# Attention and a routed expert layer on one core: the beginning of attention is ordered anew (constant rows, sums, zeros on TensorE, DMA semaphores in the plan), and x is turned later

## The chip, the core and the metric

The kernel runs on one core of a Trainium2 chip. It is one launch, and its metric is the device time of that launch in microseconds. The profile names the engines PE (TensorE, with PEld its weight loads), DVE (VectorE), ACT (ScalarE), POOL (GpSimd) and SP (SyncE, which here only issues DMAs).

## What is computed

```python
# attention: q, k, v (8, 8, 576, 64), s (8, 8, 576)
scores = q @ k.T / sqrt(64)
cum = cumsum(maximum(s, 0))
bias = -(cum[:, None] - cum[None, :])
scores = where(causal, -1e9, scores + minimum(bias, 0))
attn = softmax(scores)
x = attn @ v                      # then as (4608, 512)
# expert layer: w_gate (512, 8), w1 (8, 512, 1024), w2 (8, 1024, 512)
logits = x @ w_gate
# in falling order of logits, a token goes to its expert while it has room (576 tokens each)
out[tokens of e] = maximum(x[tokens of e] @ w1[e], 0) @ w2[e]
```

## The kernel before

The work of attention is cut into 16 groups of four heads, and a group into two pairs of heads, so there are 32 pairs, 0 to 31. For each pair there are four stages. The **maximum pass** (`spass`) multiplies q and k roughly on TensorE, and VectorE takes the maximum of each row (L471). The 20 columns of maxima are subtracted on GpSimd (L522), turned on TensorE (L524), copied by ScalarE (L526) and sent by a DMA (L529 on SP, L530 on ScalarE's queue) into rows 67 and 68 of the tile `QK`. The **score pass** (`sts`) multiplies again with these rows as part of the product (L544, L545, L547), so that the exponential on ScalarE (L555) needs no other shift; GpSimd forms the low part of each exponential (L557). `pv` multiplies with v (L621 to L623), `norm` divides, and **turn** transposes x (L684), copies it (L690) and multiplies with the gate's weights (L695, L696). When attention has ended, the tokens are routed and the eight experts run, each with its own weights.

The numbers are kept as two float16 halves. A group's q and k are loaded into `raw` (L382), scaled and rounded by ScalarE (L409, L419), the rest is formed by VectorE (L411), and DMAs move halves between the partitions of `QK` (L416). Rows 64 to 69 of `QK` hold constants and, for each group, the cumulative sums as three float16 digits, here called pieces (`sums`, L346 to L358; the pieces are put into `QK` at L397). `QK` has four slots; group 0 uses slot 0. The constant rows of slots 0 and 1 are filled by VectorE from a small vector that GpSimd makes (L285), those of slots 2 and 3 are copied by a DMA of GpSimd from slot 1 (L290), and a gap in each slot is cleared (L297 on GpSimd or L298 on VectorE). The constants of the router are made by GpSimd (L822 to L851) and at L858 to L860 by VectorE. Until the first data are there TensorE multiplies zeros (L742, `WARM` of them).

The order of the work comes from a planner (`Plan`). Each task is added with an engine, a duration in us, what it depends on and a priority (a lower number goes first); a task may also name buffers of a ring. The planner then plays the work through: it always starts the task that can start earliest, among equals the one with the lowest priority number, and writes the instructions in that order, so each engine's queue has the planned order. A ring with `ordered` set hands out its buffers in the order in which the program asked for them; the three PSUM buffers `pst` of the score pass are such a ring. A DMA's landing is planned from its size, from a shared bus (`KBUS`) and from the constants `BEGIN`, `LAND` and `LATE`. On the chip each DMA that SP or ScalarE issues uses one of eight semaphores in turn, and the issue waits until the DMA that had the semaphore before has landed.

Priorities in pairs' numbers n: maximum pass n - 3 to n - 2, its maxima n - 2.9, score pass n to n + 0.86, `pv` n + 1 to n + 1.9, `turn` n + 2.6, zeros at the beginning 50, constants of the router 3.

Of the kernel before, what the change touches and what calls it, by code (L numbers as in the profile page):

```python
# [14 lines left out]
OP = mybir.AluOpType  # L15
# [24 lines left out]
WARM = 70  # L40
# [49 lines left out]
class Plan:  # L90
# [9 lines left out]
    def __init__(self, t0=0.0):  # L100
# [5 lines left out]
        self.dma = t0  # L106

    def add(self, e, dur, f, deps=(), prio=1, takes=(), uses=(), lat=None, hold=0.0, kb=0, slack=0.0, lock=False,
            alt=None, bulk=False):
# [72 lines left out]
    def start(self, t, x, e):  # L182
# [17 lines left out]
        if x.kb:  # L200

            self.dma = max(self.dma, t + (1.0 if e == "p" else 0.0 if x.land is None else self.BEGIN)) + x.kb / self.KBUS
            x.lat = self.dma - t + (x.lat if x.land is None else x.land + self.LATE[not x.bulk])
        x.end = t + x.lat
        self.free[e] = t + x.occ
# [11 lines left out]
class Attention:  # L217
    def __init__(self, tc, ctx, qT, kT, vN, sN, wg, xs, nb, L, router=None):
# [7 lines left out]
        self.pl = Plan()  # L226
        self.rings()
# [20 lines left out]
    def consts(self):  # L248
# [5 lines left out]
        def P(name, dur, f, prio, deps=(), alt=None):  # L254
            k[name] = pl.add("p", dur, f, [k[d] for d in deps], prio=prio, alt=alt)
# [23 lines left out]
        for i in range(4):  # L279
            t = self.r["QK"].slots[i][0]  # L280
            p0 = -97 if i == 0 else 2 * i - 5.6
            rows, made = t[64:70, 0], []
            if i < 2:
                for c in (1, 0):
                    made.append(pl.add("v", 0.85, lambda rows=rows, c=c: nc.vector.tensor_scalar(  # L285
                        rows[:, c].rearrange("p r (h c) -> p (r h) c", h=2), zrow, self.vec[64:70, c:c + 1], None,
                        op0=OP.add), [k["vec", 0, 4], k["vec", 1, 1], k["mZ"]], prio=p0 if c or i else -94, lock=True))
            else:

                made.append(pl.add("p", 0.9, lambda rows=rows: nc.gpsimd.dma_start(rows, self.r["QK"].slots[1][0][64:70, 0]),  # L290
                                   self.rows1 + [k["QK", 1]], prio=-20, kb=62))
                self.moved.append(made[0])
            k["row", i] = made
            if i == 1:
                self.rows1, self.moved = made, []
# [38 lines left out]
    def sums(self):  # L334
# [12 lines left out]
                    uses=sb)  # L347
        V = lambda dur, f, deps: pl.add("v", dur, f, deps, prio=-95, lock=True, uses=sb)
# [14 lines left out]
    def load(self, g):  # L363
# [22 lines left out]
        if g == 1:  # L386
            fresh = fresh + self.moved
# [17 lines left out]
        for a, z in parts:  # L405
# [4 lines left out]
                         [ld[r, t] for r in range(a, z)] + fresh[:1], prio=t0 - 5 + off + t / 10, uses=[raw, QK]) for t in range(2)]  # L410
# [4 lines left out]
            def move(to, fr, deps, o):  # L415
                return Sy(0.6, lambda d, a=a, z=z: d(part(*to, a, z), part(*fr, a, z)), deps, off=o + off, uses=[QK], kb=72 * n,  # L416
# [1195 lines left out]
```

## Time and profile before

| | |
|---|---|
| median of 3 runs | 755.11 us (754.41 to 755.82) |
| the profiled execution's own time | 760.82 us |
| its span, first to last instruction | 759.1 us |
| mean granted TensorE clock over the span | 0.973 of 2.4 GHz |
| TensorE busy | 719.3 us, 95% |
| VectorE busy | 591.0 us, 78% |
| ScalarE busy | 389.5 us, 51% |
| GpSimd busy | 339.9 us, 45% |
| attention | from 0 to about 318 us |

A row of a timeline gives the start and the length of an instruction in us, its engine, line and operation, the tile that is written and those that are read, the number of merged instructions, and in square brackets how long the engine stood idle before it and what ended that. SPq, ACTq and POOL with DMA_DIRECT2D are issues of DMAs; their length is that of the issue, not of the transfer. A row of a table by stretches gives, for each engine, the busy time and the number of instructions, and then the granted clock (1.00 is 2.4 GHz, 0.50 is 1.2 GHz) and the DMA engines' share.

### The profile page before, as it was taken

What the parts mean: (1) busy time and instruction counts of PE and PEld (TensorE: products, weight loads), DVE (VectorE), ACT (ScalarE), POOL (GpSimd) and SP (SyncE); (2) the same over time, 40 slices, a digit from 0 to 9 for tenths busy, and PEclk for the clock granted to TensorE, in tenths of its full rate; (3) what the DMA queues carried; (4) which work ended last, traced back from release to release, by engine and by line L of the source; (5) the groups of instructions that cost most, each with busy time, mean ns of one, the idle gap of its engine ahead of it and who ended that gap; (6) DMA issues with size and microseconds to landing.
All of it is one profiled execution on the core that took longest, in us unless ns stands there. A gap on an engine that the chain in (4) does not pass through costs nothing.

```text
span 759.1 us, 22699 instructions
## 1 busy us (share of the span) xinstructions
PE 719.3 (95%) x8799; PEld 458.8 (60%) x8799; DVE 591.0 (78%) x1955; ACT 389.5 (51%) x793; POOL 339.9 (45%) x449
## 2 busy tenths in 40 slices
PE   8799999999999999757999999999999999999997
PEld 3467778788888888647645545445455454454444
DVE  8989999999999997878887968879689796260110
ACT  3658888898888878505334414333234332351111
POOL 7667988878788889403031050320312223201102
PEclk9889999999999999858999999999999999999999
DMA  7897768677767431206177383773837749930001
GB/s 231 223 226 190 230 164 240 188 230 200 216 186 215 108 87 65 66 23 218 48 204 186 112 187 113 212 198 115 220 100 167 201 159 240 267 112 32 32 15 50
DMA packets 90838, 119.00 MB, mean 157 GB/s; under 512 B 40350, under 2 KB 56862, under 8 KB 90718
## 3 DMA queue, kind: packets, MB, share of 16 engines
q1 hardware_dynamic: 84172, 98.08, 47.2%
q0 software_dynamic: 6000, 19.01, 8.8%
q8 instruction: 69, 1.13, 0.6%
q10 hardware_dynamic: 558, 0.47, 0.3%
q14 instruction: 39, 0.32, 0.1%
HBM read 71.68 MB, written 19.10 MB: 120 GB/s over the span
## 4 chain that ended last, share of the span: by engine, by line
PE 57%; issue 19%; DVE 15%; POOL 5%; DMA 2%; ACT 1%; SPq 1%; POOLq 0%; another core or an unknown queue 0%; DVEq 0%; ACTq 0%
PE psm L1407 14%; PE psm L1513 12%; DVE pss L471 5%; PE pst L545 4%; PE pst L544 4%; PE pss L502 3%; PE po L621 3%; PE po L623 3%; PE po L622 3%; POOL out_dram L1466 2%; PE psn L1411 2%; DVE QK L411 2%; PE pss L684 2%; PE psa L1084 2%; PE pst L547 1%
## 5 line engine op out<-in xcount | busy, mean ns | idle before, releaser
L557 POOL TENSOR_TENSOR R<-P 128x512 f16<-128x512 f32 (+1 forms) x220 | 219.7, 1024 | 27.5 <-ACT P L555 25.8
L1407 PE MATMUL psm<-xT,w1p 128*128 128x512 f16 (+1 forms) x876 | 194.9, 355 | 0.7 <-ACT xT L1349 0.7
L1513 PE MATMUL psm<-w2p,hT 128*128 128x512 f16 x744 | 169.1, 379 | 0.0
L555 ACT ACTIVATE P<-pst 128x512 f32<-128x512 f32 (+1 forms) x224 | 119.9, 554 | 25.5 <-PE pst L547 10.5
L1411 PE MATMUL psn<-xT,w1p 128*128 128x64 f16 x768 | 129.7, 193 | 0.0
L1466 POOL DMA_INDIRECT out_dram<-y,ids x39 | 39.2, 1004 | 200.7 <-ACT y L1524 175.7
L1407 PEld LDWEIGHTS <-w1p 128*128 128x128 f16 x876 | 80.1, 99 | 78.3 <-issue 0.8
L471 DVE CUSTOM_DVE_ANT_0 pss<-pss,mS 128x512 f32<-128x512 f32 (+3 forms) x256 | 122.8, 507 | 5.7 <-PE pss L502 3.3
L1513 PEld LDWEIGHTS <-hT 128*128 128x128 f16 x744 | 66.8, 98 | 77.4 <-issue 4.3
L621 PE MATMUL po<-V,P 128*128 128x65 f16 x945 | 111.8, 196 | 1.1 <-DVE xp L652 0.9
L623 PE MATMUL po<-V,R 128*128 128x65 f16 x945 | 112.0, 194 | 0.0
L622 PE MATMUL po<-Vl,P 128*128 128x64 f16 x945 | 111.6, 193 | 0.0
L544 PE MATMUL pst<-QK 70*128 70x64 f16 (+4 forms) x512 | 108.3, 251 | 0.7 <-ACT P L555 0.7
L545 PE MATMUL pst<-QK 128*128 128x64 f16 (+4 forms) x512 | 107.6, 251 | 0.0
L622 PEld LDWEIGHTS <-P 128*128 128x128 bf16 x960 | 89.7, 99 | 8.3 <-issue 1.8
L1329 POOL DMA_INDIRECT xg<-xs,ids x40 | 42.2, 1056 | 116.8 <-DVE ids L1286 62.4
L1427 ACT ACTIVATE hT<-psm 128x512 f16<-128x512 f32 x64 | 38.1, 597 | 109.5 <-PE psm L1407 88.6
L621 PEld LDWEIGHTS <-P 128*128 128x128 bf16 x960 | 90.2, 98 | 6.4 <-issue 2.6
L623 PEld LDWEIGHTS <-R 128*128 128x128 f16 x960 | 89.7, 97 | 0.0
L1524 ACT ACTIVATE y<-psm 128x512 f32<-128x512 f32 x31 | 18.5, 597 | 116.7 <-PE psm L1513 106.9
L502 PE MATMUL pss<-QK 67*128 67x512 f16 (+3 forms) x256 | 71.8, 302 | 4.3 <-DVE mr L471 2.8
L1429 DVE SCALAR_TENSOR_TENSOR hT<-psm,hT 128x512 f16<-128x512 f32 x64 | 43.9, 687 | 39.6 <-ACT hT L1427 38.9
(255 smaller groups left out, 1478.1 us busy)
## 6 DMA issues: line engine op xcount, KB each, us to landing
QK<-QK SPq DMA_DIRECT2D x120, 144.0 KB
wst<-in_w_dram SPq DMA_DIRECT2D x32, 512.0 KB
wst<-in_w_dram SPq DMA_DIRECT2D x64, 256.0 KB
raw<-in_q_dram SPq DMA_DIRECT2D x32, 288.0 KB
raw<-in_k_dram SPq DMA_DIRECT2D x32, 288.0 KB
rv<-in_v_dram SPq DMA_DIRECT2D x32, 288.0 KB
xs<-xp SPq DMA_DIRECT2D x32, 256.0 KB
xs<-xp SPq DMA_DIRECT2D x8, 128.0 KB
```

Source lines behind the costliest of these rows:

```text
L471: return pl.add("v", dur, lambda: nc.vector.tensor_tensor_reduce(ps(), ps(), mask, 1.0, init() if init else -3e38, OP.add, OP.max, mr.t[:, ...
L502: nc.tensor.matmul(ps.t[:, :n], F()[:, q0:q0 + 128], F()[:, k0:k0 + n], start=True, stop=True)
L544: nc.tensor.matmul(ps[:, c0:c0 + n], F()[:, ks:ks + 128], F()[:, q:q + n], start=True, stop=False)
L545: nc.tensor.matmul(ps[:, c0:c0 + n], G()[:, ks:ks + 128], G()[:, q:q + n], start=False, stop=not diag)
L555: e = pl.add("a", n / 1200 + 0.171, lambda: nc.scalar.activation(P.t[:, c0:c0 + n], ps.t[:, :n], AF.Exp, scale=1.0 / YS), [x] + fresh, pri ...
L557: sub = lambda eng: eng.tensor_tensor(R.t[:, c0:c0 + n], P.t[:, c0:c0 + n], strided_hi(P.t)[:, c0:c0 + n], op=OP.subtract)
L621: nc.tensor.matmul(o[:, i], H[:, c:c + 128], V.t[:, pr, sl], start=f, stop=False)
L622: nc.tensor.matmul(o[:, i, 0:64], H[:, c:c + 128], Vl.t[:, pr, sl], start=False, stop=False)
L623: nc.tensor.matmul(o[:, i], R.t[:, c:c + 128], V.t[:, pr, sl], start=False, stop=l)
L1407: nc.tensor.matmul(ps[:, tiles[0]:tiles[-1] + 1] if len(tiles) > 1 else ps[:, tiles[0]], lhs(f, c, a), xT.t[:, tiles[0]:tiles[-1] + 1, 4 * ...
L1411: nc.tensor.matmul(pt.t[:, 64 * f:64 * f + 64], lhs(f, c, a), xT.t[:, 4, 4 * b + c, 0:64], start=s, stop=e)
L1513: nc.tensor.matmul(py.t, hT.t[:, f, a, 128 * i:128 * i + 128], w2p.t[:, f, b], start=f == 0 and k == 0, stop=f == 7 and k == 2)
```

## The change

- Rows: only slot 0's rows are filled by VectorE, ahead of the other constants; slots 1, 2 and 3 get theirs by DMAs of GpSimd, slot 1 from slot 0, and 2 and 3 from slot 1. The pieces of group 0 wait until the copy out of slot 0 has landed, those of group 1 until the others have. The gaps are cleared by GpSimd alone, and the conversions of q and k no longer wait for that.
- Sums: tasks marked `seq` are planned without the small pause between dependent instructions of one engine; constants of GpSimd no longer exclude locked instructions of VectorE in the plan.
- Zeros: after the maxima of pairs 0 to 3 have been turned, 10, 4, 6 and 4 matmuls of zeros go into a buffer of the score pass's ring.
- Plan of attention: a DMA's landing is planned with 0.5 us in the place of 2.0 us, and SP and ScalarE have eight transfers in flight at most. Moves of `QK` count 100 KB a head in the place of 72.
- Router's constants: the first 13 are made at the beginning, the others after the maxima of pair 0; `own` and `same` are made by GpSimd.
- `turn` has priority n + 3.4 in the place of n + 2.6.

```diff
+WARM, HALF = 70, 13
+HOT = (10, 4, 6, 4)
 # Plan
+        self.late = 2.0
+        self.lands, self.lanes = [], 0
...
-            d.next.append((x, e == d.e == "t"))
+            d.next.append((x, e == d.e == "t" or seq and e == d.e))
...
+        if x.kb and e in "sa" and 0 < self.lanes <= len(self.lands):
+            t = max(t, self.lands[-self.lanes])
...
-            x.lat = ... else x.land + self.LATE[not x.bulk])
+            x.lat = ... else x.land + self.late)
...
+        if x.kb and e in "sa":
+            self.lands.append(x.end)
 # Attention.__init__
+        self.pl.late = 0.5
+        self.pl.lanes = 8
 # consts
-            k[name] = pl.add("p", dur, f, [k[d] for d in deps], prio=prio, alt=alt)
+            k[name] = pl.add("p", dur, f, [k[d] for d in deps], prio=prio, alt=alt, seq=True)
+            k[name].lock = False
...
-            if i < 2:
+            if not i:
                 for c in (1, 0):
                     made.append(pl.add("v", 0.85, ...
-                        op0=OP.add), [...], prio=p0 if c or i else -94, lock=True))
+                        op0=OP.add), [...], prio=-99.5, lock=True))
+                self.rows, self.copied = made, []
             else:
-                made.append(pl.add("p", 0.9, lambda rows=rows: nc.gpsimd.dma_start(rows, self.r["QK"].slots[1][0][64:70, 0]),
-                                   self.rows1 + [k["QK", 1]], prio=-20, kb=62))
+                made.append(pl.add("p", 0.9, lambda rows=rows, i=i: nc.gpsimd.dma_start(rows, self.r["QK"].slots[min(i - 1, 1)][0][64:70, 0]),
+                                   self.rows, prio=-99 if i == 1 else 2, kb=62, lat=2.6))
+                self.copied.append(made[0])
...
-            k["QK", i] = pl.add("p", 1.1, lambda x=x: g.memset(x, 0.0), made, prio=p0 + 0.1,
-                                alt=("v", 0.5, lambda x=x: nc.vector.memset(x, 0.0)))
+            k["QK", i] = pl.add("p", 0.95, lambda x=x: g.memset(x, 0.0), made, prio=p0 + 0.1)
 # load
-        if g == 1:
-            fresh = fresh + self.moved
+        if g < 2:
+            fresh = fresh + self.copied[g:g + 1] + self.copied[g + 1:] * g
...
-                         [ld[r, t] for r in range(a, z)] + fresh[:1], prio=t0 - 5 + off + t / 10, ...
+                         [ld[r, t] for r in range(a, z)], prio=t0 - 5 + off + t / 10, ...
 # sts, ahead of the units of the score pass
+        if n0 < len(HOT):
+            zeros, hot, x = self.mZ.bitcast(F16)[:, 0:512], self.buf("pst"), self.turned_max
+            for _ in range(HOT[n0]):
+                x = pl.add("t", 0.22, lambda hot=hot: nc.tensor.matmul(hot.t, zeros[:, 0:128], zeros, start=True, stop=True),
+                           [x], prio=n0 + 0.95, uses=[hot])
 # turn
-        prio = 2 * g + pr + 2.6
+        prio = 2 * g + pr + 3.4
 # build
-        x = None
-        for e, dur, f in self.router.consts():
-            x = pl.add(e, dur, f, [x], prio=3)
-        self.k["router"] = x
+        todo, x = self.router.consts(), None
+        def more(n, x):
+            for e, dur, f in todo[:n]:
+                x = pl.add(e, dur, f, [x, self.k.get("router")], prio=3, seq=True)
+                x.lock = False
+            del todo[:n]
+            self.k["router"] = x
+        more(HALF, None)
...
                 self.spass(g, pr)
+                if todo:
+                    more(len(todo), self.eased)
 # Router.consts
-        do(0.29, lambda: v.tensor_reduce(self.own, one.rearrange("p j c -> p c j"), AX.X, OP.add), "v")
-        do(0.29, lambda: v.tensor_reduce(self.same1, one, AX.X, OP.add), "v")
-        do(0.29, lambda: v.tensor_copy(self.same.rearrange("p (a j) -> p a j", j=J), ...), "v")
+        do(0.2, lambda: g.tensor_add(half, self.identf[:, 0:64], self.identf[:, 64:128]))
+        for n in (32, 16):
+            do(0.2, lambda n=n: g.tensor_add(half[:, 0:n], half[:, 0:n], half[:, n:2 * n]))
+        do(0.2, lambda: g.tensor_add(self.own, half[:, 0:G], half[:, G:2 * G]))
+        do(0.35, lambda: g.affine_select(same, on..., pattern=[[0, 128 // J], [-G, J]], base=0, ...
+        do(0.35, lambda: g.affine_select(same, same, pattern=[[0, 128 // J], [G, J]], base=G - 1, ...
```

## Rows read from the trace of the kernel before

**Rows 1.** Busy time by stretch; then granted clock, DMA share and GB/s.
```profile
15.00:25.00 10.00, 7.29 (x39) 3.29 (x39) 9.16 (x35) 3.95 (x6) 3.16 (x7) 1.00 1.00 275
25.00:32.00 7.00, 6.08 (x35) 3.53 (x35) 6.93 (x15) 5.11 (x10) 4.03 (x5) 0.51 0.71 165
32.00:39.00 7.00, 4.63 (x66) 3.34 (x66) 6.47 (x20) 3.10 (x7) 6.81 (x8) 0.97 0.90 226
39.00:45.00 6.00, 6.00 (x52) 4.00 (x50) 4.91 (x19) 3.04 (x7) 2.96 (x4) 0.50 1.02 219
...
88.00:300.00 212.00, 210.17 (x4106) 173.29 (x4103) 204.10 (x680) 180.68 (x421) 176.94 (x195) 1.00 0.63 177
```

**Rows 2.** Timeline of TensorE: first score matmul of pairs 0, 1, 2, 6, 31.
```profile
26.50 0.63 PE L544 MATMUL pst<-QK 70*128 70x512 f16 x1
...
39.05 0.62 PE L544 MATMUL pst<-QK 70*128 70x512 f16 x1
...
52.47 0.38 PE L544 MATMUL pst<-QK 70*128 70x512 f16 x1
...
88.45 0.38 PE L544 MATMUL pst<-QK 70*128 70x512 f16 x1
...
304.60 0.38 PE L544 MATMUL pst<-QK 70*128 70x512 f16 x1
```

**Rows 3.** Timelines of VectorE, ScalarE, GpSimd, SP and TensorE, 0 to 16 us.
```profile
2.65 1.67 DVE L285 TENSOR_SCALAR QK<-mZ,vec 6x2560 f16<-6x2560 f16 x2
4.49 0.48 DVE L298 MEMSET QK<- 128x512 uint32 x1 [0.17 <-DVE QK L285]
5.01 0.46 DVE L349 TENSOR_SCALAR xp<-xp 64x576 f32<-64x576 f32 x1
...
8.16 0.45 DVE L355 TENSOR_SCALAR xp<-xp 64x576 f16<-64x576 f32 x1
...
9.43 1.16 DVE L358 TENSOR_SCALAR xp<-xp 64x576 f16<-64x576 f32 x1
...
4.81 0.68 ACT L409 ACTIVATE QK<-raw 128x576 f16<-128x576 f32 x1 [2.69 <-DMA raw<-in_q_dram]
...
8.75 1.53 POOL L822 IOTA k<- 128x256 bf16 x1
...
12.48 0.69 SPq L397 DMA_DIRECT2D QK<-xp  x1
...
15.19 0.66 PE L502 MATMUL pss<-QK 67*128 67x128 f16 x3
```

**Rows 4.** Timelines of VectorE, ScalarE's and SP's queues and TensorE, 21 to 49 us.
```profile
21.09 0.88 DVE L285 TENSOR_SCALAR QK<-mZ,vec 6x2560 f16<-6x2560 f16 x1
...
22.04 0.70 ACTq L530 DMA_DIRECT2D QK<-mt  x1
...
34.38 0.67 ACTq L530 DMA_DIRECT2D QK<-mt  x1
...
48.12 0.71 SPq L529 DMA_DIRECT2D QK<-mt  x1
...
25.69 1.01 PE L486 MATMUL pss<-QK 67*128 67x512 f16 x2 [1.50 <-DVE mr L471]
```

**Rows 5.** Timeline of GpSimd, 23 to 39 us.
```profile
23.29 1.31 POOL L290 DMA_DIRECT2D QK<-QK  x2 [0.31 <-POOL QK L297]
27.47 0.95 POOL L297 MEMSET QK<- 128x1024 f16 x1 [2.86 <-DMA QK<-QK]
...
31.00 7.72 POOL L557 TENSOR_TENSOR R<-P 128x512 f16<-128x512 f32 x6
```

**Rows 6.** Timeline of TensorE: the zeros of the beginning.
```profile
1.62 13.44 PE L742 MATMUL po<-mZ 128*128 128x512 f16 x55 [1.62 <-DVE mZ L258]
```

**Rows 7.** Timelines of VectorE at 30 us and TensorE at 316 us.
```profile
29.70 0.38 DVE L858 TENSOR_REDUCE own<-identf 128x8 f32<-128x128 f32 x1
...
316.12 0.57 PE L684 MATMUL pss<-ident,xp 128*128 128x128 f16 x5
```

More of the change, by code (lines that the diff above doesn't have):

```diff
@@ L202, in start @@
             self.dma = max(self.dma, t + (1.0 if e == "p" else 0.0 if x.land is None else self.BEGIN)) + x.kb / self.KBUS
-            x.lat = self.dma - t + (x.lat if x.land is None else x.land + self.LATE[not x.bulk])
+            x.lat = self.dma - t + (x.lat if x.land is None else x.land + self.late)
         x.end = t + x.lat
+        if x.kb and e in "sa":
+            self.lands.append(x.end)
         self.free[e] = t + x.occ
@@ L280, in consts @@
             t = self.r["QK"].slots[i][0]
-            p0 = -97 if i == 0 else 2 * i - 5.6
+            p0 = -86.5 if i == 0 else 2 * i - 5.6
             rows, made = t[64:70, 0], []
-            if i < 2:
+            if not i:
                 for c in (1, 0):
@@ L409, in load @@
             hi = [pl.add("a", dur, lambda t=t, a=a, z=z: act(part(A_, 1, t, t, a, z), raw.t[:, t, a:z], AF.Copy, scale=QS),
-                         [ld[r, t] for r in range(a, z)] + fresh[:1], prio=t0 - 5 + off + t / 10, uses=[raw, QK]) for t in range(2)]
+                         [ld[r, t] for r in range(a, z)], prio=t0 - 5 + off + t / 10, uses=[raw, QK]) for t in range(2)]
             lo = [pl.add("v", 0.15 + n * S / 960, lambda t=t, a=a, z=z: stt(
@@ L415, in move @@
             def move(to, fr, deps, o):
-                return Sy(0.6, lambda d, a=a, z=z: d(part(*to, a, z), part(*fr, a, z)), deps, off=o + off, uses=[QK], kb=72 * n,
+                return Sy(0.6, lambda d, a=a, z=z: d(part(*to, a, z), part(*fr, a, z)), deps, off=o + off, uses=[QK], kb=100 * n,
                           both=True)
@@ L419, in load @@
                 e1 = [pl.add("a", dur, lambda t=t, a=a, z=z: act(part(E_, 0, t, 0, a, z), raw.t[0:64, t, a:z], AF.Copy,
-                                                                 scale=QS), [ld[r, t] for r in range(a, z)] + fresh[:1],
+                                                                 scale=QS), [ld[r, t] for r in range(a, z)],
                              prio=t0 - 4.9 + off + t / 10, uses=[raw, QK]) for t in range(2)]
@@ L527, in spass @@
                    uses=[ps, mt])
+        self.turned_max = x
         to = QK
@@ L825, in consts @@
         for n, f in enumerate(self.forms):
[L826 to L828 removed]
+            f.kj = iota([128, f.J, f.G], [[1, f.J], [0, f.G]], base=1, dt=BF, name=f"kj{n}", dur=0.45)
+        self.k7 = iota([128, 1, 128, 2], [[0, 1], [1, 128], [0, 2]], base=1, dt=BF, name="k7", dur=1.5)
+        self.i32 = iota([128, 32, 4], [[1, 32], [0, 4]], dt=BF, name="i32", dur=0.5)
         self.row = iota([128, 2, 5, 4], [[S, 2], [128, 5], [0, 4]], base=-2 * S, cm=1, dt=F16, name="row")
@@ L855, in consts @@
         self.g7 = c.tile([128, EARLY // 2, 128, 2], F16, name="g7")
-        self.own, self.same1, self.same = T([128, G], F32, "own"), T([128, J], F32, "same1"), T([128, 128], F16, "same")
-        v, one = nc.vector, self.identf.rearrange("p (j c) -> p j c", c=G)
-        do(0.29, lambda: v.tensor_reduce(self.own, one.rearrange("p j c -> p c j"), AX.X, OP.add), "v")
-        do(0.29, lambda: v.tensor_reduce(self.same1, one, AX.X, OP.add), "v")
-        do(0.29, lambda: v.tensor_copy(self.same.rearrange("p (a j) -> p a j", j=J),
-                                       self.same1[:, None, :].to_broadcast([128, 128 // J, J])), "v")
+        self.own, self.same = T([128, G], F32, "own"), T([128, 128], F16, "same")
+        half = T([128, 64], F32, "half")
+        do(0.2, lambda: g.tensor_add(half, self.identf[:, 0:64], self.identf[:, 64:128]))
+        for n in (32, 16):
+            do(0.2, lambda n=n: g.tensor_add(half[:, 0:n], half[:, 0:n], half[:, n:2 * n]))
+        do(0.2, lambda: g.tensor_add(self.own, half[:, 0:G], half[:, G:2 * G]))
+        same = self.same.rearrange("p (a j) -> p a j", j=J)
+        do(0.35, lambda: g.affine_select(same, on.rearrange("p (a j) -> p a j", j=J), pattern=[[0, 128 // J], [-G, J]], base=0,
+                                         channel_multiplier=1, compare_op=OP.is_ge, fill=0.0))
+        do(0.35, lambda: g.affine_select(same, same, pattern=[[0, 128 // J], [G, J]], base=G - 1,
+                                         channel_multiplier=-1, compare_op=OP.is_ge, fill=0.0))
         fill(self.U, 1.0)
```

21 lines of the change are left out of this document (9 added, 12 removed).

## The prediction

> **What bounds the kernel now.** I read the stretches first. From 88 to 300 us TensorE is busy 210.2 of 212 us at the full granted clock, and VectorE 204.1 [rows 1]: attention's steady stretch is TensorE's, with VectorE close behind. In the first 45 us it is otherwise. The granted clock is 0.51 from 25 to 32 us and 0.50 from 39 to 45 us (the lower level, 1.2 GHz), although TensorE is busy 6.08 and 6.00 us there, and both times an idle stretch stands before it: 7.29 us busy of 10 ahead of the first, with zeros counted as work, and 4.63 of 7 ahead of the second [rows 1].
>
> Then I laid the score passes of the pairs beside each other in the timeline of TensorE [rows 2]. The pass of pair 6 starts at 88.45 us and that of pair 31 at 304.60, so a pair takes 216.15/25 = 8.65 us. Pairs 0 to 6 take 88.45 - 26.50 = 61.95 us where six steady pairs would take 51.9. **10.05 us** are lost between pair 0 and pair 6, and whatever comes before 26.50 us is lost whole. About 1.5 us of the 10.05 is no loss: the maximum pass has got one more pair ahead by then (3712 columns at 2.4 GHz by the code, an estimate). As the steady stretch leaves TensorE no slack, an earlier pair 6 is an earlier end, and what follows attention isn't touched.
>
> What holds the first pair? VectorE fills the constant rows of slot 0 (2.65 us), clears its gap (4.49) and starts the sums at 5.01; the last digit ends at 10.59 (9.43 + 1.16); SP issues a piece of it at 12.48, and the first maximum matmul starts at 15.19 [rows 3]. Its maxima are sent at 22.04 us, and the score pass starts at 26.50. The maxima of pairs 1 and 2 are sent at 34.38 and 48.12 and used at 39.05 and 52.47 [rows 2, 4]: 4.46, 4.67 and 4.35 us from issue to use. So in the first pairs the score pass waits for that transfer, while TensorE has little else.
>
> **The change, part by part.**
>
> *Rows and sums.* VectorE loses the two fills of slot 1 (0.88 us each, one of them at 21.09 in the middle of the maximum pass [rows 4]) and slot 0's memset (0.48 us [rows 3]). The fills go ahead of the other constants, so they can start some 0.5 us earlier. Then the sums start at 5.01 - 0.5 - 0.7 = 3.8 us, if `s` is there; its landing isn't shown. A piece of q twice as large, issued 0.65 us later, is used at 4.81 [rows 3], so 3.8 to 4.8 are the ends and I take 4.2: -0.8. The last conversion takes 1.16 us and the same operation before it 0.45, and GpSimd's long iota runs from 8.75 to 10.28 [rows 3]; nothing in the change keeps the two apart, so 0 to -0.7, taken -0.6, as the iota gets another place. The last digit comes 1.4 us earlier, at 9.2. From digit to piece SP spends 12.48 - 10.59 = 1.9 us on other issues; with the DMA semaphores in the plan I take 0.7 of it back (0 to 1.3). **First maximum pass: -2.1 us** (0 to -3.4), at 13.1.
>
> *The copy of the rows.* It is a new wait: every piece now waits for GpSimd's transfer from slot 0 to slot 1. On SP and ScalarE what is queued behind a piece is the moves of pair 0 and the conversions of q and k. The nearest rows are the two old copies: issued at 23.29, and the memset that waits for the first starts at 27.47 [rows 5], so 4.2 us. Issued after the fill, at some 4.5 us, it lands at 8.7, just before the digits: 0, with +1.5 as the other end, as the raw loads then fill the queues. The row of the iota shows that VectorE and GpSimd can hold each other up. The Trainium skill (SBUF — State Buffer, "Who interferes with whom") says more: a DMA issued by GpSimd has its descriptors held back while VectorE runs certain one-input operations, and the sums are partly such. By that rule the copy would land later by the length of those operations; no row here shows it for a copy. As a mechanism it is the third rival.
>
> *From maximum to scores, pair 0.* The fill of 0.88 us at 21.09 is gone from VectorE's queue, and the two matmuls at 25.69, which wait 1.50 us for VectorE, stand in TensorE's queue in front of the scores [rows 4]. The transfer bounds the gain, as its three spacings lie within 0.32 us: 0 to -1.9, taken **-1.0**. Score pass 0 starts at 23.4.
>
> *Zeros.* 24 matmuls (10, 4, 6, 4) of 13.44/55 = 0.244 us or less [rows 6], 5.9 us at most, stand between the turned maxima and the scores of pairs 0 to 3. Where TensorE waits for the transfer they cost nothing; if that cover is gone they cost their whole length. At the full level the two slow stretches would hold half as much TensorE time: (6.08 + 6.00)/2 = 6.0 us saved. Not all reaches the end, as GpSimd's subtractions run without a gap from 31.00 to 38.72 [rows 5] and the clock doesn't shorten them. Ends 0 and -6.0, taken half: **-3.0**.
>
> *Router constants.* The three operations from 29.70 on leave VectorE (0.38 us the first, 1.1 in all by it, at a time when it is busy 6.93 of 7 us [rows 1, 7]); that is within the -3.0. On GpSimd the rest of the list waits for pair 0's maxima: about ten operations more than before, an estimate of 5 us in all by the iota and the memset of rows 3 and 5, in the 2.86 us and more that it now stands idle. If they slip in front of a subtraction, score passes wait for scores: 0 taken, +2 the end.
>
> *The plan's transfers.* A transfer is thought to land 1.5 us earlier than before, and no more than eight from SP and ScalarE are in flight. The order of every queue can move. In the steady stretch transfers are issued long ahead, so 0, from -1 to +2; in the first pairs see the fourth rival.
>
> *x turned later.* Ten transposes (0.57 us for five [rows 7]) and the gate's dots change places. Only at the end of attention can they stick out: 0 to +0.9, taken **+0.3**.
>
> **Sum:** -2.1 - 1.0 - 3.0 + 0.3 = -5.8 us. The profiled execution took 760.82 us (its span 759.1, so 1.7 around it) and would take 755.0; it lies 5.7 above the median of the runs, so from 755.11 the forecast is **749.3 us**. VectorE allows it: it loses 0.88 + 1.1 us on the path and starts 2.1 earlier, and it had 0.84 + 0.07 + 0.53 us idle from 15 to 39 [rows 1].
>
> **The rivals.**
> 1. *The clock still falls.* A gap ahead of pair 0's or 2's scores stays, and the zeros stand at the wrong place, as the plan fixes their number before the transfers are known. For it: before pair 0's maxima there were zeros too, and the clock fell. Then -5.8 + 3.0 = -2.8: **752.3**.
> 2. *Slower: the zeros hold back the scores.* They take one of the three PSUM buffers of the score passes, in a ring that hands them out in order, and until the last zero has run two are left. If at pairs 0 to 3 other matmuls are ready, or the buffer is missed, the 24 zeros cost 5.9 us and the clock's gain is eaten by it: -2.8 + 5.9 = +3.1, **758.2**. It decides from the point where TensorE has no gap between the turned maxima and the landing. Against it: 7.29 of 10 and 4.63 of 7 us [rows 1].
> 3. *The copy is late* and the pieces go when they went before: the first -2.1 is lost, **751.4**. For it: the old copy's 4.2 us, with slack of 0.5 us only.
> 4. *No change.* The plan puts score passes where it thinks the maxima have landed; measured, it takes 4.35 us or more. What stands behind them in TensorE's order then waits some 1.5 us (the plan's new shortening) in each of four pairs: -5.8 + 6.0, **755.3**. Against it: the zeros stand in just that wait.
>
> **How the numbers follow.** Forecast 0.50 (its own range 746 to 752), clock 0.18, slower 0.14, late copy 0.08, no change 0.10. A measurement of this kernel tells 0.2%, 1.5 us, from no change; rival 1 lies 1.3 us from that bound, so 0.04 of it counts as no change. Faster 0.50 + 0.14 + 0.08 = 0.72, within 0.14, slower 0.14. The range goes from 744.5 (the far ends of the start and of the clock, together) to 757.5, just short of the second rival.
>
> **What would show it.** Right: the first maximum matmul near 13 us, the first scores near 23.5, no stretch at 0.50 before 60 us, score pass 6 near 82, and from there 8.65 us a pair. Wrong: pieces that wait for the copy; zeros with busy matmuls on both sides and scores right behind them; a pair in the steady stretch over 8.7 us.

## The result, and the profile after

The changed kernel takes **766.42 us** (764.34 to 769.80, six runs) beside 756.00 us of the kernel before in the same rounds: a ratio of **1.0132**, 95% interval 1.0092 to 1.0172. It is slower by about 10 us; 749.3 was forecast, 744.5 to 757.5 the range.

Where the time went shows in the row that [rows 2] began with, the first score matmul of a pair. The timeline of TensorE in the kernel after, pairs 0, 1, 2, 6, 9 and 31:

```profile
28.14 0.38 PE L557 MATMUL pst<-QK 70*128 70x512 f16 x1
...
38.47 0.38 PE L557 MATMUL pst<-QK 70*128 70x512 f16 x1
...
46.58 0.38 PE L557 MATMUL pst<-QK 70*128 70x512 f16 x1
...
88.13 0.38 PE L557 MATMUL pst<-QK 70*128 70x512 f16 x1
...
115.71 0.38 PE L557 MATMUL pst<-QK 70*128 70x512 f16 x1
...
312.00 0.38 PE L557 MATMUL pst<-QK 70*128 70x512 f16 x1
```

And pair 9 in the timeline of the kernel before:

```profile
115.71 0.38 PE L544 MATMUL pst<-QK 70*128 70x512 f16 x1
```

Pair 9 starts at 115.71 us in both. By then TensorE has issued the same work in both, but for one matmul fewer of each kind of PV in the kernel after (240 for 241), ten transposes fewer of the late `turn` (60 for 70), and the 24 zeros. So the whole new beginning is worth nothing by then. From pair 6 to pair 31 a pair takes (312.00 - 88.13)/25 = **8.95 us** in the place of 8.65, so pair 31 is 312.00 - 304.60 = **7.4 us** late. That is most of the 10.4 us. What follows pair 31 took 450.6 us after and 454.5 before in these two profiled executions; before's lay 5.7 us above its median, so these two can't place the last 3 us.

The stretches of [rows 1] again, in the kernel after (busy time of TensorE, its weight loads, VectorE, ScalarE, GpSimd; granted clock, DMA share, GB/s):

```profile
15.00:25.00 10.00, 10.00 (x43) 4.26 (x42) 7.74 (x30) 1.10 (x4) 8.05 (x19) 0.71 0.70 150
25.00:32.00 7.00, 6.68 (x54) 3.75 (x52) 4.42 (x13) 3.37 (x8) 4.77 (x16) 1.00 0.74 205
32.00:39.00 7.00, 6.25 (x47) 3.16 (x45) 4.02 (x19) 4.82 (x8) 5.81 (x7) 1.00 0.93 267
39.00:45.00 6.00, 5.47 (x88) 4.13 (x86) 5.97 (x17) 3.31 (x9) 4.89 (x5) 1.00 0.79 193
...
88.00:300.00 212.00, 204.92 (x3922) 166.72 (x3921) 206.26 (x667) 171.95 (x405) 176.59 (x187) 1.00 0.65 181
```

The zeros did what they are for: the two stretches at 0.51 and 0.50 are at 1.00 now, and the lower level stands in one place, 14.0 to 20.9 us. But in the steady stretch TensorE is busy 210.17 - 204.92 = 5.25 us less, and VectorE is now the busier of the two. The chain of waits of 88 to 300 us by line says the same, first the kernel after, then the kernel before (the view cuts such a line off at its end):

```profile
by line: DVE pss L482 21.3%; DVE QK L422 9.0%; DVE Vl L455 6.2%; issue 5.3%; PE pst L558 5.0%; PE pst L557 4.9%; PE pss L513 4.7%; PE po L639 4.0%; DVE mr L482 3.9%; DMA QK<-QK 3.8%; PE po L641 3.6%; PE po L640 3.6%; DVE po L666 3.5%; DVE x
```

```profile
by line: PE pst L545 11.3%; PE pst L544 11.2%; PE pss L502 9.4%; DVE pss L471 8.6%; PE po L621 8.1%; PE po L623 7.4%; PE po L622 7.3%; PE pss L684 4.6%; PE pss L486 3.8%; PE pst L547 3.7%; issue 3.4%; DVE QK L411 3.4%; DVE po L648 2.6%; DVE
```

TensorE's score matmuls led the chain before; now VectorE's maxima (L482) and the low halves of q, k and v that it forms (L422, L455) do. The low halves have become longer too. Groups of VectorE's instructions, 88 to 290 us, after and before (count | busy us, mean ns of one):

```profile
L422 DVE SCALAR_TENSOR_TENSOR QK<-raw,QK 128x1152 f16<-128x1152 f32 x22 | 34.4, 1567 | 0.0
L455 DVE SCALAR_TENSOR_TENSOR Vl<-rv,V 128x1152 f16<-128x1152 f32 x11 | 17.7, 1612 | 0.0
```

```profile
L411 DVE SCALAR_TENSOR_TENSOR QK<-raw,QK 128x1152 f16<-128x1152 f32 x22 | 31.3, 1421 | 0.0
L444 DVE SCALAR_TENSOR_TENSOR Vl<-rv,V 128x1152 f16<-128x1152 f32 x12 | 17.5, 1455 | 0.0
```

The same instruction takes 146 and 157 ns longer, 22 x 0.146 + 11 x 0.157 = 4.9 us of VectorE in 202 us. GpSimd's subtraction (128x512) went from 1116 to 1170 ns. No edit touches either.

The beginning, in the timelines of VectorE, GpSimd, SP, ScalarE and TensorE of the kernel after; they answer to [rows 3]:

```profile
8.93 0.45 DVE L369 TENSOR_SCALAR xp<-xp 64x576 f16<-64x576 f32 x1
...
13.93 0.76 DVE L422 SCALAR_TENSOR_TENSOR QK<-raw,QK 128x576 f16<-128x576 f32 x1 [2.54 <-ACT QK L420]
...
6.94 0.75 POOL L301 DMA_DIRECT2D QK<-QK  x1
11.32 0.95 POOL L308 MEMSET QK<- 128x1024 f16 x1 [3.64 <-DMA QK<-QK]
...
11.34 2.72 SPq L408 DMA_DIRECT2D QK<-xp  x4
...
11.35 1.81 ACTq L408 DMA_DIRECT2D QK<-xp  x2
13.21 0.68 ACT L420 ACTIVATE QK<-raw 128x576 f16<-128x576 f32 x1 [4.83 <-issue]
...
23.44 0.21 ACT L529 ACTIVATE mp<-mr 128x10 f16<-128x10 f32 x1 [7.92 <-DMA QK<-QK]
...
24.98 0.71 ACTq L543 DMA_DIRECT2D QK<-mt  x1
...
14.73 0.80 PE L513 MATMUL pss<-QK 67*128 67x256 f16 x3 [3.29 <-DVE QK L422]
...
26.85 1.46 PE L566 MATMUL pst<-mZ 128*128 128x512 f16 x6
28.14 0.38 PE L557 MATMUL pst<-QK 70*128 70x512 f16 x1
```

The last digit ends at 9.38 us (forecast 9.2). But the copy of the rows is issued at 6.94, behind `ident`, `mp` and `identb` on GpSimd, and its landing releases GpSimd at 11.32 and the pieces at 11.34. ScalarE's next conversion (L420) stands behind the pieces in its queue and starts at 13.21; VectorE and TensorE wait for it in turn. TensorE stands idle for 3.29 us before the first maximum matmul. And six zeros run up to the first scores.

### The profile page after: what moved, and what is told of

It is laid out like the page before. It is cut to its first block, busy times and chain, and to the rows that moved or that the text cites. A ratio compares the mean times of both kernels' runs of the same rounds, so it can differ in the third digit from the quotient of the medians.

```text
span 762.6 us, 22709 instructions
## 1 busy us (share of the span) xinstructions
PE 723.1 (95%) x8823; PEld 458.1 (60%) x8823; DVE 594.5 (78%) x1942; ACT 387.7 (51%) x792; POOL 351.1 (46%) x465
## 4 chain that ended last, share of the span: by engine, by line
PE 45%; DVE 24%; issue 16%; DMA 6%; POOL 4%; SPq 2%; ACT 2%; POOLq 0%; ACTq 0%; DVEq 0%
PE psm L1437 14%; PE psm L1543 12%; DVE pss L482 9%; DVE QK L422 4%; POOL out_dram L1496 2%; DVE Vl L455 2%; PE pst L557 2%; PE pst L558 2%; PE psn L1441 2%; DVE mr L482 2%; PE pss L513 2%; DMA QK<-QK 2%; PE po L639 2%; POOL xg L1359 2%; DVE po L666 1%
## 5 line engine op out<-in xcount | busy, mean ns | idle before, releaser
L575 POOL TENSOR_TENSOR R<-P 128x512 f16<-128x512 f32 (+1 forms) x221 | 228.7, 1060 | 39.0 <-ACT P L573 34.8
L573 ACT ACTIVATE P<-pst 128x512 f32<-128x512 f32 (+1 forms) x224 | 117.3, 549 | 25.0 <-PE pst L558 8.1
L482 DVE CUSTOM_DVE_ANT_0 pss<-pss,mS 128x512 f32<-128x512 f32 (+3 forms) x256 | 122.1, 506 | 6.7 <-PE pss L513 5.6
L557 PE MATMUL pst<-QK 70*128 70x64 f16 (+4 forms) x512 | 105.9, 246 | 0.3 <-ACT P L573 0.3
L558 PE MATMUL pst<-QK 128*128 128x64 f16 (+4 forms) x512 | 104.4, 246 | 0.0
L1459 DVE SCALAR_TENSOR_TENSOR hT<-psm,hT 128x512 f16<-128x512 f32 x64 | 43.9, 687 | 34.1 <-ACT hT L1457 33.3
```

Source lines behind the costliest of these rows:

```text
L482: return pl.add("v", dur, lambda: nc.vector.tensor_tensor_reduce(ps(), ps(), mask, 1.0, init() if init else -3e38, OP.add, OP.max, mr.t[:, ...
L557: nc.tensor.matmul(ps[:, c0:c0 + n], F()[:, ks:ks + 128], F()[:, q:q + n], start=True, stop=False)
L558: nc.tensor.matmul(ps[:, c0:c0 + n], G()[:, ks:ks + 128], G()[:, q:q + n], start=False, stop=not diag)
L573: e = pl.add("a", n / 1200 + 0.171, lambda: nc.scalar.activation(P.t[:, c0:c0 + n], ps.t[:, :n], AF.Exp, scale=1.0 / YS), [x] + fresh, pri ...
L575: sub = lambda eng: eng.tensor_tensor(R.t[:, c0:c0 + n], P.t[:, c0:c0 + n], strided_hi(P.t)[:, c0:c0 + n], op=OP.subtract)
```

## The experiments

The expectations use these names. **T**: the later `turn` costs the steady stretch. **P**: the new prices of transfers do. **B**: something else of the change does (copies, zeros, constants; also new planned durations of some of GpSimd's constants, as 0.55 for 0.35 us, and of the landing of `s`). **O**: any new order of the queues loses it, whatever made it new; the kernel before has an order that suits this stretch. Within O, for how an order costs time: **S**, GpSimd's reads meet VectorE's two-input operations more often and both get longer; **W**, waits between queues.

All runs at a glance; "pair 6", "pair 31": first score matmul, us. The ratio is to the kernel before on the same chip; the other columns come from one profiled execution each.

| run | ratio (95%) | pair 6 | pair 31 | us a pair |
|---|---|---|---|---|
| before | | 88.45 | 304.60 | 8.65 |
| after | 1.0132 (1.0092 to 1.0172) | 88.13 | 312.00 | 8.95 |
| e1_turn | 1.0221 (1.0201 to 1.0241) | 89.22 | 316.14 | 9.08 |
| e2_oldplan | 1.0064 (1.0040 to 1.0088) | 92.58 | 311.48 | 8.76 |
| e3_both | 1.0143 (1.0117 to 1.0169) | 91.88 | 313.87 | 8.88 |
| e4_before_turn | 1.0163 (1.0146 to 1.0179) | 91.70 | 321.71 | 9.20 |
| e5_before_prices | 1.0134 (1.0060 to 1.0208) | 92.33 | 317.41 | 9.00 |
| e6_before_turn27 | 1.0103 (1.0057 to 1.0150) | 88.24 | 309.90 | 8.87 |
| e7_before_bus | 1.0162 (1.0123 to 1.0200) | 83.52 | 317.21 | 9.35 |
| e12_hybrid | 1.0104 (1.0072 to 1.0136) | 87.84 | 313.98 | 9.05 |
| e13_light_before | 0.9979 (0.9923 to 1.0034) | 90.66 | 302.96 | 8.49 |
| e14_light_after | 1.0065 (1.0041 to 1.0090) | 91.07 | 309.00 | 8.72 |
| e17_unread_before | 0.9917 (0.9890 to 0.9944) | 86.86 | 298.87 | 8.48 |
| e18_unread_after | 1.0009 (0.9984 to 1.0034) | 85.71 | 302.61 | 8.68 |
| e15_zeros_before | 1.0017 (0.9992 to 1.0042) | 89.36 | 305.46 | 8.64 |
| e16_nocopy | 1.0094 (1.0064 to 1.0124) | 91.15 | 315.63 | 8.98 |
| e8_nohot | 1.0191 (1.0159 to 1.0223) | 86.59 | 319.02 | 9.30 |
| e19_after_begin | 1.0094 (1.0066 to 1.0122) | 93.45 | 311.90 | 8.74 |
| e20_before_begin | 1.0109 (1.0082 to 1.0137) | 89.35 | 315.87 | 9.06 |
| e21_bus_begin | 1.0085 (1.0053 to 1.0116) | 92.91 | 309.03 | 8.65 |

### The turn and the prices, taken out and put in alone

```diff
 e1, in after             -prio = 2 * g + pr + 3.4
                          +prio = 2 * g + pr + 2.6
 e2, in after             -self.pl.late = 0.5
                          -self.pl.lanes = 8
                          -... uses=[QK], kb=100 * n
                          +... uses=[QK], kb=72 * n
 e3, in after             the edits of e1 and e2
 e4, in before            -prio = 2 * g + pr + 2.6
                          +prio = 2 * g + pr + 3.4
 e5, in before            late = 0.5, lanes = 8, kb = 100 * n
```

> The changed kernel with one number put back: turn has priority n + 2.6. Theory T (the late turning of x slows the steady stretch): a pair takes about 8.65 us from pair 6 to pair 31 again, in the place of 8.96, and the time falls by some 7 us or more below the changed kernel, to about 757. Theory P (the new prices of transfers in the plan order the steady stretch worse): the pair stays at 8.9 to 9.0 us and the time within 2 us of the changed kernel. Both predict the beginning up to pair 6 as in the changed kernel, 88 us.

> The changed kernel with the plan's prices of transfers put back: 2.0 us for 0.5, no limit of eight in flight, 72 KB for 100 a head. Theory P: 8.65 us a pair, time about 757 or less, as the beginning's rows, sums and zeros stay. Theory T: the pair stays at 8.9 to 9.0 us and the time near 766. If the zeros or the new beginning are the cause, neither this nor the run with the old turn priority comes below 8.9 us a pair.

> The changed kernel with both put back, turn priority and prices of transfers; rows, sums, zeros and router constants stay as changed. Theories T and P alike: 8.65 us a pair and a time at or below the kernel before, 750 to 757. Theory B (the beginning itself shifts the order of the steady stretch): a pair still takes 8.85 us or more.

> The kernel before with one number changed: turn has priority n + 3.4. Theory T: 8.9 us a pair or more and a time of some 762 to 766. Theory P: 8.65 us a pair, within 2 us of the kernel before.

> The kernel before with the prices of transfers of the changed kernel (0.5 us, eight in flight, 100 KB a head) and nothing else. Theory P (the prices order the steady stretch worse): a pair takes 8.9 us or more from pair 6 to 31 and the time is 760 or above; the beginning is earlier, score pass 6 at 88 or below. Theory O (the kernel before has an order that happens to suit the steady stretch, and any new order of the queues loses it): also 8.75 us a pair or more, so this run alone does not part the two. If prices are harmless: 8.65 us and a time at or below 755.

Putting the late turn in alone costs pace (9.20), as T has it, but taking it out of the kernel after costs pace as well (9.08). The prices in alone cost pace too (9.00); out of the kernel after, the pace is better (8.76) and the ratio 1.0064 for 1.0132, but it isn't back at 8.65. With both out (e3) it is 8.88, which is what B had forecast. So neither T nor P is needed for the loss, and the four paces are no sum of effects: this is what led to O.

### Edits without a meaning

```diff
 e6, in before            -prio = 2 * g + pr + 2.6
                          +prio = 2 * g + pr + 2.7
 e7, in before            -KBUS = 270.0
                          +KBUS = 272.0
 e12, in after            new late and lanes only while the planned time is under 50 us (100 KB a head stays)
```

> The kernel before with turn's priority n + 2.7 in the place of n + 2.6: an edit without meaning, which still gives other queues. Theory O: 4 to 12 us slower than the kernel before, 8.75 us a pair or more. Theories T and P: within 2 us of the kernel before, 8.65 us a pair.

> The kernel before with the plan's bus at 272 in the place of 270 GB/s: again an edit without meaning (a transfer of 288 KB is planned 8 ns shorter), which gives other queues. Theory O: 4 to 12 us slower, 8.75 us a pair or more. Theories T and P: within 2 us of the kernel before.

> The changed kernel with its new prices of transfers only as long as the plan's clock is below 50 us, and the old ones after. Theory P: the beginning as in the changed kernel (score pass 6 near 88 us) and then 8.65 to 8.75 us a pair, a time of 754 to 760. Theory O: the beginning as changed, then any pace from 8.7 to 9.1 us a pair, without a rule.

A priority of 2.7 for 2.6 costs 1.0%, a planned DMA rate of 272 for 270 GB/s costs 1.6%: as much as the whole change. Neither adds or removes work, and e7 touches nothing that the change touches. The planner takes at each step what it thinks can start first, so a difference of hundredths of a microsecond early on can give another order for all that follows. e12, with the old `late` and no limit in flight from 50 us on, didn't get the old pace back (9.05), as O has it.

### The orders exchanged

The planner of e19, e20 and e21 chooses for itself up to the score pass of pair 5; from there it starts the tasks in the order recorded from the other kernel.

```diff
 Plan.run
+            if self.todo and self.turned:
+                waiting = {y.rank: y for w in self.wait.values() for y in w}
+                for n, (rank, e) in enumerate(self.todo):
...
+                self.start(t, x, e)
+                continue
 e19: beginning of after, order of before
 e20: beginning of before, order of after
 e21: beginning of e7, order of before
```

> The changed kernel as it is up to the score pass of pair 5; from there the planner no longer chooses, but starts the tasks in the order in which the kernel before starts them (the list stands in the kernel; a task that cannot start yet is passed over until it can, and the order has come together again with that of before by about pair 8). Theory O (the order of the queues in the steady stretch is what the change lost): from pair 8 on 8.65 us a pair as before, in the place of 8.95, and the whole 7 us shorter than the changed kernel, a ratio to before of 0.997 to 1.004. Rival (something else of the change sets the pace: its copies, its zeros, the moment at which the stretch is reached): 8.95 us a pair and 1.010 to 1.014.

> The other half of the exchange: the kernel before as it is up to the score pass of pair 5, and from there the order of the changed kernel. None of the change's edits is in it. Theory O: 8.95 us a pair from pair 8 on and a ratio to before of 1.008 to 1.013. Rival: 8.65 us a pair and 0.998 to 1.002.

> The beginning with the earliest pair 6 of all runs (the kernel before planned with 272 GB/s in the place of 270: 83.52 us, against 88.45) up to the score pass of pair 5, and from there the order of the kernel before. Theory O: 8.65 us a pair, and if the early pair 6 is not paid for with work put off, 4.9 us less than before: a ratio of 0.993; with work put off up to 1.000. Rival (a beginning fixes the pace of what follows): 9.3 us a pair as in that run and 1.016.

First scores of pairs 9 and 31 in the timeline of TensorE, of e19, e20 and e21:

```profile
121.88 0.38 PE L665 MATMUL pst<-QK 70*128 70x512 f16 x1
...
311.90 0.38 PE L665 MATMUL pst<-QK 70*128 70x512 f16 x1
```

```profile
117.84 0.38 PE L652 MATMUL pst<-QK 70*128 70x512 f16 x1
...
315.87 0.38 PE L652 MATMUL pst<-QK 70*128 70x512 f16 x1
```

```profile
120.17 0.38 PE L651 MATMUL pst<-QK 70*128 70x512 f16 x1
...
309.03 0.38 PE L651 MATMUL pst<-QK 70*128 70x512 f16 x1
```

Over these 22 pairs: 8.64, **9.00** and 8.58 us a pair; the kernel before makes 8.59, the kernel after 8.92. So the pace goes with the order, whichever kernel began. By the timelines TensorE's 3693 matmuls from pair 9 to pair 31 stand in e19 and e21 in exactly the order of the kernel before (by tile and shape), and e20's 3696 in that of the kernel after; the work done by pair 9 and by pair 31 is therefore the same within an order. With e15 below, the old order ran in four profiled executions at 8.58 to 8.64 and the new one in two at 8.92 and 9.00. The low halves go with it too (groups of VectorE, 88 to 290 us, e19 and e20):

```profile
L530 DVE SCALAR_TENSOR_TENSOR QK<-raw,QK 128x1152 f16<-128x1152 f32 x22 | 31.3, 1421 | 0.0
```

```profile
L519 DVE SCALAR_TENSOR_TENSOR QK<-raw,QK 128x1152 f16<-128x1152 f32 x22 | 33.5, 1526 | 0.0
```

1421 ns in e19 is the very value of the kernel before; 1526 in e20 is near the 1567 of the kernel after. This **shows** for the pace that the order sets it. B falls: e19 has the copies, the zeros and the constants and the old pace, e20 has none of them and the new one. T and P work through the order alone, and the recorded order of after contains the late turn, so these three runs don't part them from O. What speaks against them as the cause are e3, which has neither and stays at 8.88, and e7, which has none of the change's edits and loses most.

The totals of e19 and e21 miss, though. In e19 pair 9 is 6.2 us later than in either kernel. Of that, 82.57 - 78.85 = 3.7 us are there at pair 5, where its order is still that of after, and e20, run on the same chip with before's order up to pair 5, is as late there (80.17 against 76.57); 2.5 us come at the seam. In e21 the seam is worse:

```profile
76.00 0.38 PE L651 MATMUL pst<-QK 70*128 70x512 f16 x1
...
92.91 0.38 PE L651 MATMUL pst<-QK 70*128 70x512 f16 x1
```

From pair 5 to pair 6 it takes 16.91 us where e7 itself took 7.97. Its early pair 6 was borrowed: work that the other order wants done by then was still to do. So the forecasts of a ratio near 1 for e19 and e21 failed, and O is shown for the pace and not for the whole time. No run joined a shorter beginning with the old pace, and none that computes everything beats the kernel before.

### How an order costs time

```diff
 e13, e14                 -eng.tensor_tensor(R.t[...], P.t[...], strided_hi(P.t)[...], op=OP.subtract)
 (before, after)          +eng.tensor_copy(R.t[...], P.t[...])
 e17, e18                 -eng.tensor_tensor(R.t[...], P.t[...], strided_hi(P.t)[...], op=OP.subtract)
 (before, after)          +eng.memset(R.t[...], 0.0)
```

> The kernel before with GpSimd's subtraction of the low parts (L557) replaced by a plain copy of the exponentials into R: the low parts are left out. Its planned duration stays, so every queue has the order of the kernel before. Theory S (what the new orders lose is that GpSimd's two-input operation runs against VectorE's, and both get longer): little changes here, 8.5 to 8.65 us a pair, as this order has few such meetings (1.01 us a subtraction, 1.43 us a low half of q and k). Theory W (the new orders lose by waits between TensorE, ScalarE and VectorE in their queues): likewise.

> The changed kernel with the same replacement, its queues as in the changed kernel; the low parts are left out. Theory S: the low halves of VectorE fall from 1.57 to about 1.4 us, and a pair from 8.96 to within 0.1 us of the light kernel before. Theory W: a pair keeps 0.2 us or more over the light kernel before.

> The kernel before with GpSimd's subtraction replaced by a memset of R to zero, which reads nothing and waits for no exponential; the low parts are left out. The queues keep their order. Theory S (the pace is lost where GpSimd's reading operation runs against VectorE's two-input ones): the low halves of q and k take about 1.3 us and a pair 8.4 to 8.5 us. Theory W (it is lost by waits between the queues): the same here.

> The changed kernel with the same replacement, queues as in the changed kernel; the low parts are left out. Theory S: the low halves take about 1.3 us here too, and a pair comes within 0.08 us of the kernel before with this replacement; what stayed with the copy (8.72 against 8.49) were the copy's own meetings. Theory W: a pair keeps 0.15 us or more, and TensorE's and VectorE's idle time stays above that of the other.

These four kernels leave the low parts out and serve for the pace alone. The queues stay as they are; only GpSimd's work on `R` gets shorter and, in e17 and e18, reads nothing and waits for no exponential. With the copy (e13, e14) the paces stand 8.72 - 8.49 = 0.23 us apart: more than S allowed, within what W asked. VectorE's low halves in the steady stretch, e17 and e18:

```profile
L411 DVE SCALAR_TENSOR_TENSOR QK<-raw,QK 128x1152 f16<-128x1152 f32 x21 | 28.2, 1345 | 0.0
```

```profile
L422 DVE SCALAR_TENSOR_TENSOR QK<-raw,QK 128x1152 f16<-128x1152 f32 x22 | 29.6, 1348 | 0.0
```

Equal now, and shorter than in either kernel, so GpSimd's subtraction is what lengthened them. The traces show the meetings themselves. From 88 to 290 us a low half of q and k that a subtraction covers for under 5% of its time takes 1331 ns in the kernel before and 1349 after (ten and five of them); one that is covered for over 60% takes 1541 and 1704 ns (six and twelve). In all, subtractions cover 35% of the low halves' time before and 60% after, so in the new order the two meet more often: S is shown as a mechanism. But the two paces still stand 8.68 - 8.48 = 0.20 us apart, of 0.31. About a third of the gap went with the subtraction, and not all of that need be S, as the memset also waits for no exponential. What remains shows where TensorE's share is read in the same stretch, e17 and e18:

```profile
88.00:300.00 212.00, 212.00 (x4219) 176.50 (x4215) 199.66 (x686) 183.50 (x429) 82.78 (x205) 1.00 0.62 175
```

```profile
88.00:300.00 212.00, 209.05 (x4094) 172.34 (x4091) 198.93 (x671) 176.39 (x419) 81.41 (x200) 1.00 0.66 184
```

TensorE has no idle time in e17 and 2.95 us in e18, with the same work a pair in another order. That is W: over some 24 pairs it makes 0.12 of the 0.20 us; the other 0.08 isn't placed. In the kernel after itself the waits of TensorE from 97 to 312 us name VectorE (us in total, times, longest):

```profile
PE pss L513 <- DVE den L665: 1.9, 4, 0.6
PE po L713 <- DVE xp L670: 1.7, 3, 1.0
PE pss L513 <- DVE mr L482: 1.3, 4, 0.4
```

In the kernel before the longest such sum is 0.9 us:

```profile
PE po L621 <- DVE xp L652: 0.9, 2, 0.6
```

Single waits weren't removed, so what each is worth stays open.

### The beginning

```diff
 e15, in before           7 zeros behind the turned maxima of pair 0 and 7 ahead of the last product of pair 1's maximum pass, unknown to the plan
 e16, in after            rows of slot 1 filled by VectorE as before; no piece of group 0 waits for a copy
 e8, in after             -HOT = (10, 4, 6, 4)
                          +HOT = ()
```

> The kernel before with 14 matmuls of zeros (7 behind the turning of pair 0's maxima, 7 ahead of the last product of pair 1's maximum pass) that the plan doesn't know of, so that all queues keep their order. If the clock of the beginning is worth what the prediction took (half of 6 us): no stretch at 0.5 from 25 to 32 us, score pass 6 some 3 us earlier than 88.45, then 8.65 us a pair, and 3 us faster than the kernel before. Theory O allows that too, as the order is kept; if a mere shift in time of the beginning already spoils the steady stretch, the pace rises above 8.75 us a pair though the order is the same.

> The changed kernel with slot 1's rows filled by VectorE again, so that pair 0's pieces wait for no copy. If the copy is what held the beginning: pieces from about 9.4 us instead of 11.34, the first maximum matmul at about 12.5 instead of 14.73, the first scores 2 us or more earlier than 28.14. If not: 14 to 15 us as before. The steady stretch gets a new order, so by theory O its pace is anywhere from 8.7 to 9.3 us.

> The changed kernel without the 24 zeros ahead of the first score passes. If the zeros keep the clock up: stretches at 0.5 come back between 25 and 50 us and score pass 6 starts 2 us or more later than 88.13. If they only hold the scores back: the first scores earlier than 28.14 and score pass 6 earlier. By theory O the pace of the rest is again anywhere from 8.7 to 9.3 us a pair.

e15 keeps before's order and its pace (8.64), the control to e6 and e7. Its zeros took away the lower level at 25 us; it stands at 34.1 to 47.7 us instead, as long as the two stretches before together, and nothing is gained (1.0017, where 3 us were expected).

e16 shows the copy's price: the first maximum matmul starts at 11.54 us, 3.2 earlier. The first scores don't follow (29.88). Its maxima are ready on ScalarE at 21.23; then GpSimd's timeline has

```profile
23.37 0.95 POOL L308 MEMSET QK<- 128x1024 f16 x1 [3.93 <-DMA QK<-QK]
24.29 0.21 POOL L533 TENSOR_TENSOR mp<-ms,mp 128x10 f16<-128x10 f32 x1
```

A clearing of a gap waits 3.93 us for a copy of rows, and the one short subtraction that the scores need (L533) stands behind it in GpSimd's queue. So with slot 1's copy gone from the front, the wait for the copies of the next slots took its place.

e8 has none of the 24 zeros, and the lower level at 36.7 to 43.5 us again and once more at 67.4 to 70.8. Its pair 6 is earlier than after's (86.59), but at pair 9 (115.78 us) it has done 15 fewer matmuls of each of the three kinds of PV, 6 fewer maximum matmuls and 5 fewer turns than after, and TensorE had been idle for 14.9 us against 9.1. Its pace, 9.30, is that of a third order.

## Why the prediction was wrong

**What failed** is the term "the plan's transfers ... In the steady stretch transfers are issued long ahead, so 0, from -1 to +2", with the step ahead of it that an earlier pair 6 is an earlier end. The text had named the danger ("the order of every queue can move") and then priced the transfers alone. What the runs showed in its place is the new order of the steady stretch: **+7.4 us** at pair 31, outside the term's bounds; e19, e20 and e21 show that the pace goes with the order. It isn't the prices' own doing, as e3, without them, still takes 8.88 us a pair. No rival had it either: the one that was slower lay in the first four pairs. The sign that was named for it, a pair over 8.7 us, is what came. The other part of the miss is the beginning: of the forecast -5.8 us nothing is left at pair 9 (115.71 us in both). With some 3 us that aren't placed, that is the way from -5.8 to +10.4.

**TensorE's lack of slack** was read rightly [rows 1], but taken as fixed. It was a property of one order: in the new one TensorE is idle for 7.1 of the same 212 us, and VectorE, at 204.1 us before and 206.3 now, leads the chain of waits.

**First maximum pass, -2.1.** 14.73 for 13.1: -0.5. The digits came as worked out (9.38 for 9.2), the last conversion at 0.45 us away from the iota. The copy was costed at 0, "issued after the fill, at some 4.5 us"; it was issued at 6.94 because of what stands ahead of it on GpSimd. Its length was about right: 4.2 us by [rows 5], 11.32 - 6.94 = 4.4 measured. That is the late copy of the third rival, but by its issue, 2.4 us late in GpSimd's queue; the length leaves little for what VectorE ran.

**Maximum to scores, -1.0.** From issue to use 28.14 - 24.98 = 3.2 us in the place of 4.46 [rows 2, 4]: -1.3. But the stage as a whole, from the first maximum matmul to the first scores, came out 13.41 - 11.31 = +2.1 us, and the first scores at 28.14 for a forecast of 23.4, because the maximum pass itself had become longer: 14.73 to 23.44 against 15.19 to 20.46, where ScalarE takes up the maxima in the kernel before:

```profile
20.46 0.21 ACT L518 ACTIVATE mp<-mr 128x10 f16<-128x10 f32 x1 [0.82 <-DVE mr L471]
```

The clock is at the lower level for most of it (14.0 to 20.9 us), after TensorE's 3.29 us without work. That isn't the main part. e8 has the same 72 matmuls in the same order up to there, at the full level, and its pass still takes 22.06 - 14.53 = 7.5 us, so some 1.2 of the 3.4 us are the clock's:

```profile
14.53 0.49 PE L513 MATMUL pss<-QK 67*128 67x256 f16 x3 [3.69 <-DVE QK L422]
...
17.16 0.22 PE L513 MATMUL pss<-QK 67*128 67x128 f16 x1 [0.42 <-DMA QK<-QK]
...
22.06 0.21 ACT L529 ACTIVATE mp<-mr 128x10 f16<-128x10 f32 x1 [6.74 <-DVE mr L482]
```

TensorE waits there at 17.16 us for a move of `QK`, and the moves stand behind the pieces in the queues. How much of the other 2.2 us that makes, no run parts.

**Zeros and clock, -3.0.** The clock came back where it was forecast, and fell in another place, as the first rival had it: 6.8 us at the lower level remain of 13.6 (25.0 to 31.8 and 38.6 to 45.4 before). The sum at TensorE, for 0 to 116 us, after and before:

```profile
0.00:116.00 116.00, 106.90 (x1505) 73.38 (x1506) 102.87 (x323) 77.05 (x168) 90.74 (x142) 0.97 0.75 201
```

```profile
0.00:116.00 116.00, 105.23 (x1494) 74.05 (x1495) 108.38 (x338) 79.20 (x171) 87.75 (x127) 0.94 0.79 211
```

The clock gives (13.6 - 6.8)/2 = 3.4 us (by the rounded 0.97 and 0.94, 3.5), less idle time 106.90 - 105.23 = 1.7; the 24 zeros take 24 x 0.216 = 5.2 (six in 1.46 us, one alone 0.38, so (1.46 - 0.38)/5 each). Together that is -0.1, an estimate, where pair 9 measured 0.0; it takes every zero as uncovered and leaves out the ten transposes that the kernel after hasn't done by then (about 2 us). The second rival's mechanism, zeros without cover, was there: they run with matmuls on both sides, at a price (5.2 us by the estimate) near its 5.9. But it isn't what made the kernel slower, as the two are level at pair 9.

**Pair 6 as the yardstick.** Pair 2 of the kernel after starts 52.47 - 46.58 = 5.9 us earlier, and pair 3 0.4 us later than before. When pair 2 starts, after has done 15 PV matmuls of a kind for before's 45, and 49 maximum matmuls for 57. The lead was an order, not progress.

**Router's constants, late turn.** Nothing in the runs prices them by themselves: an edit that the plan sees can change the order too.

**Sums.** The far ends of the first pass's parts add up to -3.2 us, not -3.4, and the far ends of the start and the clock with the other terms as taken give 745.0, not 744.5. Neither bears on the miss.

## What to carry to other kernels

Where a planner or a list scheduler writes the queues, a small edit anywhere is an edit of the whole order: test it beside one or two edits that mean nothing, and don't credit an edit with what they do too. A change that is meant for the beginning should leave the order behind it alone. And compare two orders where the work done is counted to be equal, not where one kind of matmul first appears.

## What the runs showed that was not expected

- One instruction of VectorE, two inputs and 1152 elements, takes 1346 ns where GpSimd's memsets cover it for over 60% of its time (eight in e18) and 1541 to 1704 ns where subtractions do (kernels before and after). The Trainium skill (SBUF — State Buffer, "Who interferes with whom") says that a VectorE instruction with two SBUF inputs contends with a GpSimd instruction that reads SBUF, and not with one that only writes; these two kernels agree with it on the first count and e18 on the second. e17 tells nothing here, as no memset of it meets such an instruction.
- GpSimd's side pays as well. Its subtraction takes 1037 and 1040 ns, before and after, where it meets next to no low half, and 1884 and 1697 (7 and 23 of them) where low halves cover it for 50 to 90%; the one and the three that lie almost whole within a low half aren't longer. The mean went from 1116 to 1170. A memset of the same tile takes 524 or 525 ns in e18, covered or not.
- The same order of the beginning isn't equally long in every profiled execution: pair 5 came 3.6 and 3.7 us later in e20 and e19 than in the profiles of the kernels whose beginnings they have, and the median of the kernel before was between 755.3 and 761.5 us from one chip to another. The ratios are against runs on the same chip for that reason.
